# Attention and FFN on one core: the first unit's denominators at the end of a visit, VectorE's conversions, sums and transpositions between its slots

## The chip, the cores and the metric

The kernel runs on one core of one Trainium2 chip. Its inputs and outputs are fp32. The metric is the device time of one execution in microseconds (us), of which several runs are taken; their median is compared.

## The reference

Attention with normalized queries and keys over 8 batches of 12 heads, 448 tokens and 64 channels a head, and behind it a feed-forward network (FFN) with a squared ReLU over all 3584 tokens:

```python
def rmsnorm(x, g):
    return x / np.sqrt(np.mean(x * x, axis=-1, keepdims=True) + 1e-06) * g
q_n, k_n = rmsnorm(q, g_q), rmsnorm(k, g_k)
scores = 1.0 / np.sqrt(q.shape[-1]) * np.matmul(q_n, k_n.transpose(0, 1, 3, 2))
attn = np.exp(scores - np.max(scores, axis=-1, keepdims=True))
attn = attn / (np.sum(attn, axis=-1, keepdims=True) + 1e-09)
attn_out = np.matmul(attn, v)                                # (8, 12, 448, 64)
x = attn_out.transpose(0, 2, 1, 3).reshape(8 * 448, 12 * 64) # (3584, 768)
h = np.maximum(x @ w_in, 0.0)                                # w_in (768, 2048)
out = h * h @ w_out                                          # w_out (2048, 768)
```

## The kernel before, in words

**Pairs and units.** The attention is worked off in 48 pairs, each of one batch and two heads. Two batches (12 pairs, 896 tokens) make a unit, and each unit is followed by its share of the FFN. While the attention of a unit runs, TensorE also works on the FFN of the unit before it: the FFN's matmuls are a stream (a generator) that is stepped in portions between the *visits* of the attention. Up to pair 12 a pair has two visits, and there is little to fill in between. From pair 13 on there is one visit per pair, `visit_whole(i)` (L1826). The visits 13 to 24, beside which the stream of the first FFN runs, are the "first unit" here: `first` is true in them.

**One visit.** Visit `i` finishes pair `i-1` and begins pair `i`. It has three slots, one per chunk of 128 keys. In each, TensorE multiplies pair `i-1`'s weights with the values (`attend_halves`, L569, eight matmuls) and then makes pair `i`'s scores (`score`, L451, eight matmuls); ScalarE takes the exponentials from the bank to the tiles `wT` (`weigh`, L470). The 64 keys that are left over (448 = 3·128 + 64) are done for two pairs at once: in even visits their scores (L462), in odd visits their share of the result (`attend_both`, L590). ScalarE and VectorE join the two halves of the result in `xT` (`join_halves`: L580 and L581 on ScalarE, L578 or L582 on VectorE).

**Denominators.** GpSimd adds the weight tiles of a pair to a tile `sum` (`add_up`, L489); these additions are queued behind the visit in which the weights were made. In the next visit, as its first step, `denominators(i-1)` multiplies the two sums with ones (L624, four matmuls) into the bank that `sums_bank` names, and `take_sums` has VectorE transpose that bank to the tile `inverse` (L666). The bank is bank 2. The slots' scores go to banks (0, 1), (2, 0) and (1, 2) (`banks_of`, L439), so the second slot needs bank 2 back and waits for L666. Behind the visit the tasks `invert` (VectorE, L683 and L684) and `finish` (GpSimd, L712) divide `xT`.

**What runs between the visits.** `run` (L1631) takes one step of the FFN's stream at a time: a product of six matmuls of L1025 in the first half of a block (`first_products`), matmuls of L1290 and L1204 in the second. With each it does one *deep step* (a difference or sum of parts of the weights that VectorE makes, L1516, and that SP stores; the first of these steps only stores five raw parts, L1506 and L1508), one weight sum (`make_sum`, L1556, in turn on VectorE and GpSimd), `end_join` (VectorE, L1480), some tasks, and when it is due a conversion: `convert` (L1562) has SP load a piece of the weights into one of three tiles `words` (L1428, L1433), ScalarE split it (L1447, L1448, L1450) and VectorE join it in two steps (L1461, L1480). A `words` tile comes free when L1480 has read it; a load for which none is free holds up SP and all that is queued behind it. The four tiles `more` of the deep steps come free when SP's stores (L1534) have read them.

**SP's queue.** Transfers for the attention stand in a queue of their own in the program, `transfers`, of which `follow_transfers` sends two (or some more, as the queue is longer) with each step of the stream (L333): queries and keys (`load_qk`), queries brought to another order through DRAM, values `vt` and `lasts` (`load_v`).

**Transpositions and their scaling.** `turn_blocks` (L371) transposes the next pair's keys and queries on VectorE (L374), and ScalarE scales the queries (`scale_turned`, L384). These tasks are queued ahead of the visit, two per visit; what is left of them is run at the visit's start. While `closing` is true the scaling waits until the visit's end.

Of the kernel before, what the change touches and what calls it, by code (L numbers as in the profile page):

```python
# [26 lines left out]
NJ = 3  # L27
# [198 lines left out]
def program(ctx, tc, rows, v, g, wide, ones, moe_w_in, moe_w_out, out, shift):  # L226
# [3 lines left out]
    B, H, S, D = v.shape  # L230
# [46 lines left out]
    def whole(i):  # L277
        return i > 2 * NPAIR

    def by_two(i):  # L280

        return i >= 2 * 2 * NPAIR
# [21 lines left out]
    def alone(i):  # L304

        return pairs[i][0] < 2
# [76 lines left out]
            dst = to_scale.popleft()  # L383
            nc.scalar.mul(dst, dst, g)  # L384

    to_scale, closing = deque(), False

    def load_v(i):
        b, c = pairs[i]
# [136 lines left out]
                nc.vector.tensor_copy(out=tiles[NJ][e][mine, part], in_=tr[mine, NJ, :size])  # L526

    def sums_bank(i):
        return banks[4 + (i + 1) % 2 if alone(i) else 2 if whole(i + 1) else 3][:, 0:S]

    def values_bank(i):
# [1294 lines left out]
    def visit_whole(i):  # L1826
        nonlocal closing
        late = [some for some in tasks if getattr(some, "args", None) == (i,)]
        for some in late:
            tasks.remove(some)  # L1830
        run_all()
        if shift:
            attend_all(i - 1)
            if i <= last:
                weigh_slots(i, 1)
        else:
            if not by_two(i - 1):
                denominators(i - 1)
            elif i % 2 == 0:
                both_denominators(i - 2)  # L1840
            for n in range(NJ):
                attend(i - 1, (n,))
                forget(i - 1, (n,))
                if i <= last:
                    score(i, n)
                    weigh(i, n)
                while n == 1 and i % 2 == 0 and late:
                    late.pop(0)()
            if i % 2:
                attend(i - 1, (NJ,))  # L1850
                forget(i - 1, (NJ,))
            join_halves(i - 1)
            if not by_two(i - 1):
                tasks.append(lambda: invert(i - 1))
                tasks.append(lambda: finish(i - 1))
            elif i % 2 == 0:
                tasks.append(lambda: invert_both(i - 2))
            if i % 2 == 0:
                if i <= last:
                    score(i, NJ)  # L1860
                    weigh(i, NJ)
            if i <= last:
                additions(i)
        closing = False
        scale_turned()
        tasks.extendleft(reversed(late))
        if late:
            tasks.extendleft([gap] * 3)
        if shift or i % 2:
            prepare(i + 3)  # L1870
        else:
            tasks.append(lambda: tasks.append(lambda: prepare(i + 3, 0)))
        if i <= last:
            tasks.appendleft(lambda: load_v(i))
# [7 lines left out]
    with tc.manual_schedule(engines=ENGINES):  # L1882
# [8 lines left out]
        for i in range(len(pairs) + 1):  # L1891
            for n in range(1 if whole(i) else VISITS):
# [7 lines left out]
                run(place(u, x - (1 if whole(i - 1) else 0.5)))  # L1900
                if i < last:
                    if whole(i) and not shift:
                        tasks.append(partial(lambda i: turn_blocks(i + 1, 1), i))
                        tasks.append(partial(lambda i: turn_blocks(i + 1, 0), i))
                        tasks.append(partial(lambda i: load_qk(i + 4), i))
                    else:
                        for some in (1, 0) if whole(i) else (1 - n,):
                            turn_among(i + 1, some)
                        if n or whole(i):
                            tasks.append(lambda i=i: load_qk(i + 4))  # L1910
                    if n and first and x > 1 and not shift:
                        denominators(i - 1)
# [49 lines left out]
```

## Time and profile before

| | |
|---|---|
| times of three runs, us | 1408.22, 1413.85, 1414.09 (median 1413.85) |
| profiled execution, us | 1409.54, of which its span is 1407.4 |
| busy TensorE matmul | 1352.2 us, 96% of the span |
| busy VectorE, ScalarE, GpSimd | 823.2, 619.2 and 807.1 us |
| DMA | 229.85 MB, mean 163 GB/s |

The profile is of one execution; its times are in microseconds from the start of its span. PE is TensorE's matmul, DVE is VectorE, ACT is ScalarE, POOL is GpSimd, SPq is the queue in which SP issues DMAs. In a row of the timeline stand the start, the duration of the group, engine, line and operation, the tiles written and read, the shape and the number of instructions; in brackets the idle time before them and what ended it. In a row of the list of waits stand the engine and line that waited, for whom, the microseconds in total, how often, and the longest one. In a row of the table of stretches stand the stretch and its length, then the busy time (and number of instructions) of PE, of its weight loads, of DVE, ACT and POOL, then the granted clock of TensorE (1.00 is full), DMA's busy share and GB/s. Visit 13 stands at 140 us in the profile, visit 24 at 483 us, and a visit comes every 28 to 38 us between them.

### The profile page before, as it was taken

Reading aid. Unit: us, or ns where it says so; the run is one execution under the profiler, and the core shown is the slowest. Engines: PE = TensorE matmul, PEld = TensorE weight load, DVE = VectorE, ACT = ScalarE, POOL = GpSimd, SP = SyncE. Lnnn points to the kernel's source line nnn. Section 1 sums busy time; section 2 is a strip of 40 time slices with the busy share of each in tenths; the row PEclk is TensorE's granted clock in tenths of the full one; section 3 lists DMA queues with packets and bytes.
Section 4 is the critical chain, followed back from the end, with each engine's and each line's share of the span. In section 5 each row is a group of like instructions: output and inputs, shape, how many; then the busy total and the mean of one; then the engine's idle time right before and its main releaser. Section 6 shows DMA issues by size and latency. Waiting matters only on the chain.

```text
span 1407.4 us, 20180 instructions
## 1 busy us (share of the span) xinstructions
PE 1352.2 (96%) x6608; PEld 855.0 (61%) x6608; DVE 823.2 (58%) x1647; ACT 619.2 (44%) x1136; POOL 807.1 (57%) x804
## 2 busy tenths in 40 slices
PE   7997999899899899999999999999999999999998
PEld 3332455354344458585867667676858686868684
DVE  4897446676566775455555775555545742444444
ACT  6994567656657324343334434343433132303030
POOL 5668656565546696576576888567545740303030
PEclk9999999999999999999999999999999999999999
DMA  5665746767767858384756766584717361616133
GB/s 140 162 186 147 198 107 159 227 193 187 213 172 222 245 160 254 80 232 115 190 144 162 240 172 201 123 223 94 235 33 258 113 207 38 199 38 199 38 124 103
DMA packets 394374, 229.85 MB, mean 163 GB/s; under 512 B 271892, under 2 KB 355988, under 8 KB 393236
## 3 DMA queue, kind: packets, MB, share of 16 engines
q1 hardware_dynamic: 393968, 228.41, 57.7%
q8 instruction: 54, 0.88, 0.3%
q14 instruction: 60, 0.49, 0.1%
q10 hardware_dynamic: 292, 0.07, 0.0%
HBM read 171.05 MB, written 57.34 MB: 162 GB/s over the span
## 4 chain that ended last, share of the span: by engine, by line
PE 78%; DVE 8%; issue 4%; DMA 3%; POOL 3%; SPq 2%; ACT 1%; POOLq 0%; DVEq 0%; ACTq 0%
PE bank L1290 29%; PE bank L1081 25%; PE bank L451 6%; PE bank L569 6%; PE bank L1025 4%; PE bank L462 2%; PE bank L1204 2%; DVE acc L1387 1%; PE bank L590 1%; PE bank L554 1%; PE bank L624 1%; PE bank L633 1%; POOL rr L204 1%; DVE more L1516 1%; DVE out_sb L1480 1%
## 5 line engine op out<-in xcount | busy, mean ns | idle before, releaser
L1081 PE MATMUL bank<-xT,in_sb 128*128 128x224 f32 x1344 | 287.9, 353 | 0.1
L1290 PE MATMUL bank<-out_sb,hid 128*128 128x384 f32 x768 | 275.3, 490 | 12.4 <-DVE acc L1387 9.8
L1081 PEld LDWEIGHTS bank<-xT,in_sb 128*128 128x128 f32 x1344 | 252.9, 190 | 10.5 <-ACT wT L470 5.8
L1387 DVE TENSOR_TENSOR acc<-acc,bank 128x384 f32<-128x384 f32 x312 | 165.7, 547 | 129.6 <-PE bank L1290 118.7
L470 ACT ACTIVATE wT<-bank,rr 128x448 f32<-128x448 f32 x288 | 165.3, 631 | 155.6 <-PE bank L451 140.1
L1290 PEld LDWEIGHTS bank<-out_sb,hid 128*128 128x128 f32 x768 | 144.6, 190 | 115.8 <-DVE acc L1387 15.1
L1290 PE MATMUL bank<-out_sb,sums 128*128 128x384 f32 x576 | 207.9, 492 | 2.5 <-DVE acc L1387 2.0
L204 POOL TENSOR_TENSOR rr<-ms,minus_half 128x8 f32<-128x8 f32 (+1 forms) x96 | 146.3, 1524 | 64.7 <-DVE ms L197 62.1
L1290 PEld LDWEIGHTS bank<-out_sb,sums 128*128 128x128 f32 x576 | 108.4, 191 | 87.4 <-issue 5.5
L1066 DVE TENSOR_TENSOR hid<-hid,bank 128x224 f32<-128x224 f32 x312 | 111.3, 383 | 84.1 <-PE bank L1081 78.8
L451 PE MATMUL bank<-qT,kT 64*64 64x448 f32 x840 | 119.6, 551 | 10.1 <-DVE inverse L666 8.6
L1025 PE MATMUL bank<-xT,in_sb 128*128 128x448 f32 x336 | 128.7, 542 | 0.0
L489 POOL TENSOR_TENSOR sum<-sum,wT 128x448 f32<-128x448 f32 (+1 forms) x96 | 114.7, 1213 | 1.9
L489 POOL TENSOR_TENSOR sum<-wT 128x448 f32<-128x448 f32 x48 | 53.7, 1138 | 108.0 <-ACT wT L470 108.0
L569 PE MATMUL bank<-wT,vt 64*64 64x448 f32 x864 | 113.4, 551 | 0.0
L1025 PEld LDWEIGHTS bank<-xT,in_sb 128*128 128x128 f32 x336 | 63.1, 190 | 66.5 <-issue 65.2
L1134 POOL TENSOR_TENSOR hid<-hid 128x448 f32<-128x448 f32 x24 | 27.3, 1143 | 123.2 <-DVE hid L1066 118.2
L1138 ACT ACTIVATE hid<-hid 128x448 f32<-128x448 f32 x96 | 55.0, 573 | 72.0 <-DVE hid L1066 48.1
L582 DVE TENSOR_TENSOR xT<-xT,bank 128x448 f32<-128x448 f32 x36 | 22.4, 621 | 102.1 <-ACT xT L581 99.5
L451 PEld LDWEIGHTS bank<-qT,kT 64*64 64x64 f32 x840 | 45.8, 134 | 55.8 <-issue 38.2
L384 ACT ACTIVATE qT<-qT,g 128x448 f32<-128x448 f32 x34 | 22.6, 665 | 121.3 <-DVE qT L374 121.3
L1081 PE MATMUL bank<-more,in_sb 128*128 128x224 f32 x288 | 74.4, 353 | 0.0
(142 smaller groups left out, 2091.8 us busy)
## 6 DMA issues: line engine op xcount, KB each, us to landing
out_sb<-out_forms SPq DMA_DIRECT2D x80, 384.0 KB, 4.9
in_sb<-in_deep SPq DMA_DIRECT2D x64, 384.0 KB, 4.0
in_sb<-in_deep SPq DMA_DIRECT2D x80, 256.0 KB, 3.9
words<-in_moe_w_in_dram SPq DMA_DIRECT2D x32, 384.0 KB, 3.6
words<-in_moe_w_out_dram SPq DMA_DIRECT2D x32, 384.0 KB, 3.7
out_forms<-out_sb SPq DMA_DIRECT2D x8, 1536.0 KB, 6.5
qk<-in_q_dram SPq DMA_DIRECT2D x96, 96.0 KB, 2.7
qk<-in_k_dram SPq DMA_DIRECT2D x96, 96.0 KB, 2.6
```

Of the source, the lines that this page charges most:

```text
L204: self.nc.gpsimd.tensor_tensor(out=self.rr[i][:, x, 0 : self.count(i)], in0=ms, in1=self.minus_half.to_broadcast(list(ms.shape)), op=ALU.pow,)
L451: nc.tensor.matmul(sc[ds(half * D, D)], lhsT=turned[i, 1][ds(e * D, D), ds(m * P + half * D, D)], rhs=turned[i, 0][ds(e * D, D), :], start ...
L462: nc.tensor.matmul(sc[some], lhsT=turned[p, 1][r, keys], rhs=turned[p, 0][r, :], start=True, stop=True,)
L470: nc.scalar.activation(new_weights((i, m), e), sc, AF.Exp, scale=rows.rr[i][:, 1, 2 * m + e : 2 * m + e + 1],)
L489: nc.gpsimd.tensor_tensor(out=sums[i, e][some], in0=left[some], in1=weights[key_of(i, m), e][some], op=ALU.add)
L569: nc.tensor.matmul(bank[ds(e * D, D), :], lhsT=values[i][keys, n, e, :], rhs=weights[(i, n), e][keys], start=n == 0, stop=n == NJ - 1 and ...
L1025: nc.tensor.matmul(ps, lhsT=w_sb[:, IN.index(left), c, :], rhs=forms[u, c][right], start=first and c == 0, stop=c == NK - 1, skip_group_ch ...
L1066: nc.vector.tensor_tensor(out=quarter(name, n), in0=quarter(base, n), in1=ps, op=ALU.add)
L1081: nc.tensor.matmul(ps, lhsT=left, rhs=right, start=start, stop=stop, skip_group_check=True)
L1138: nc.scalar.activation(dst, dst, AF.Relu)
L1290: nc.tensor.matmul(ps, lhsT=extra[left][:, t] if tt == NT else lefts[left][:, t, ts(tt, P)], rhs=w_sb[t][:, OUT.index(right), :], start=fi ...
L1387: nc.vector.tensor_tensor(out=acc, in0=acc, in1=ps, op=ALU.add)
```

## The change

In the first unit's visits, and there only:

1. `sums_bank` names bank 1 for the denominators in place of bank 2.
2. `denominators(i-1)`, that is L624 on TensorE and L666 on VectorE, stands at the end of the visit in place of its start: in even visits behind the leftover keys' scores, in odd ones behind L590. The tasks `invert` and `finish` are queued behind it.
3. A conversion that has begun may take its first VectorE step (L1461) at the visit's start, unless it is the first piece of its tile; and behind each of the three slots stand `end_join` (L1480), one deep step and one weight sum.
4. In the odd visits 15 to 23, the transpositions for the next pair stand behind the first and second slot in place of ahead of the visit; the scaling on ScalarE follows at the end of the visit. The loads of `load_qk(i+4)` are queued behind the visit, ahead of `load_v(i)`.

The tiles, their buffers, the arithmetic and the number of instructions stay as they are. The lines of the changed kernel are 2 higher from `sums_bank` on (L1025 is L1027 there, L624 is L626, L666 is L668), and some more behind `visit_whole`.

```diff
-    to_scale, closing = deque(), False
+    to_scale, closing, in_visit = deque(), False, deque()
...
     def sums_bank(i):
+        if whole(i + 1) and not by_two(i):
+            return banks[1][:, 0:S]
         return banks[4 + (i + 1) % 2 if alone(i) else 2 if whole(i + 1) else 3][:, 0:S]
...
         else:
-            if not by_two(i - 1):
-                denominators(i - 1)
-            elif i % 2 == 0:
+            if i % 2 == 0 and by_two(i - 1):
                 both_denominators(i - 2)
+            if first and begun and all_pieces[begun[0]][2]:
+                join_words(begun.pop())
             for n in range(NJ):
                 attend(i - 1, (n,))
                 forget(i - 1, (n,))
...
                 while n == 1 and i % 2 == 0 and late:
                     late.pop(0)()
+                if n < 2 and in_visit:
+                    in_visit.popleft()()
+                if first:
+                    end_join()
+                    if deep_to_make:
+                        deep_to_make.popleft()()
+                    make_sum()
             if i % 2:
                 attend(i - 1, (NJ,))
                 forget(i - 1, (NJ,))
             join_halves(i - 1)
+            if i % 2 == 0:
+                if i <= last:
+                    score(i, NJ)
+                    weigh(i, NJ)
             if not by_two(i - 1):
+                denominators(i - 1)
                 tasks.append(lambda: invert(i - 1))
                 tasks.append(lambda: finish(i - 1))
...
-                        tasks.append(partial(lambda i: turn_blocks(i + 1, 1), i))
-                        tasks.append(partial(lambda i: turn_blocks(i + 1, 0), i))
-                        tasks.append(partial(lambda i: load_qk(i + 4), i))
+                        steps = [
+                            partial(lambda i: turn_blocks(i + 1, 1), i),
+                            partial(lambda i: turn_blocks(i + 1, 0), i),
+                        ]
+                        loads = partial(lambda i: load_qk(i + 4), i)
+                        if first and i % 2 and x < unit:
+                            in_visit.extend(steps)
+                            closing = True
+                        else:
+                            tasks.extend([*steps, loads])
+                            loads = None
...
                     visit_whole(i)
+                    if i < last and not shift and loads:
+                        tasks.appendleft(loads)
```

How the instructions stand on an engine shows what this does to the order. First TensorE at visit 13; `bank_172` to `bank_176` are the banks 0 to 4. Before:

```order
L1025 MATMUL bank_178<-xT,in_sb 128x448 x3
L624 MATMUL bank_174<-sum,ones 64x448 x2
L569 MATMUL bank_176<-wT,vt 64x448 x2
L569 MATMUL bank_175<-wT,vt 64x448 x2
L451 MATMUL bank_172<-qT,kT 64x448 x2
...
L451 MATMUL bank_174<-qT,kT 64x448 x2
L590 MATMUL bank_176<-wT,lasts_156 64x448 x2
L590 MATMUL bank_172<-wT,lasts_157 64x448 x2
L1025 MATMUL bank_177<-xT,in_sb 128x448 x3
```

The same place of the changed kernel:

```order
L1027 MATMUL bank_178<-xT,in_sb 128x448 x3
L571 MATMUL bank_176<-wT,vt 64x448 x2
L571 MATMUL bank_175<-wT,vt 64x448 x2
L451 MATMUL bank_172<-qT,kT 64x448 x2
...
L451 MATMUL bank_174<-qT,kT 64x448 x2
L592 MATMUL bank_176<-wT,lasts_156 64x448 x2
L592 MATMUL bank_172<-wT,lasts_157 64x448 x2
L626 MATMUL bank_173<-sum,ones 64x448 x2
L1027 MATMUL bank_177<-xT,in_sb 128x448 x3
```

The denominators (L624, now L626) have moved from ahead of the slots to behind them, directly ahead of the FFN's next matmuls, and from bank 2 to bank 1.

Then VectorE at visit 17, an odd one; `words` are pieces under conversion, `more` are deep steps. Before:

```order
L1516 TENSOR_TENSOR more<-in_sb 128x512
L1480 ISA out_sb<-words,out_sb 128x768
L1461 TENSOR_SCALAR out_sb<-words 128x384
L1167 TENSOR_TENSOR hid<-bank_178,part 128x448
L1516 TENSOR_TENSOR more<-in_sb 128x512
L1556 TENSOR_TENSOR out_sb<-out_sb 128x384
L1480 ISA out_sb<-words,out_sb 128x768
L666 STREAM_TRANSPOSE inverse<-bank_174 128x448
L582 TENSOR_TENSOR xT<-xT,bank_175 128x448
L1516 TENSOR_TENSOR more<-in_sb 128x384
```

The same place of the changed kernel:

```order
L1463 TENSOR_SCALAR out_sb<-words 128x384
L374 STREAM_TRANSPOSE kT<-qk_65 128x448
L1482 ISA out_sb<-words,out_sb 128x768
L1518 TENSOR_TENSOR more<-in_sb 128x384
L374 STREAM_TRANSPOSE qT<-qk_65 128x448
L1518 TENSOR_TENSOR more<-in_sb 128x384
L584 TENSOR_TENSOR xT<-xT,bank_175 128x448
L668 STREAM_TRANSPOSE inverse<-bank_173 128x448
L1169 TENSOR_TENSOR hid<-bank_177,part 128x448
L685 RECIPROCAL few<-inverse 128x14
```

The transposition of the sums (L666, now L668) stood ahead of the join of the halves and behind a conversion's end; now it stands behind the join of the halves (L582, now L584), and five other instructions stand ahead of that join, within the visit.

Last SP between the visits 16 and 17. Before:

```order
L1433 DMA words<-in_moe_w_out_dram 128x768
L333 DMA qk_65<-q_rows 32x14x32 x2
L1433 DMA words<-in_moe_w_out_dram 128x768
L333 DMA qk_65<-q_rows 32x14x32 x2
L1506 DMA in_deep_161<-in_sb 896x1x128 x3
L1508 DMA in_deep_161<-in_sb 896x1x128 x2
L333 DMA vt<-in_v_dram 128x3x64 x2
L1433 DMA words<-in_moe_w_out_dram 128x768
```

The same place of the changed kernel:

```order
L333 DMA q_rows<-qk_65 128x3x128
L1508 DMA in_deep_161<-in_sb 896x1x128 x3
L1510 DMA in_deep_161<-in_sb 896x1x128 x2
L333 DMA q_rows<-qk_65 64x128 x2
L1435 DMA words<-in_moe_w_out_dram 128x768 x2
L333 DMA qk_65<-q_rows 32x14x32 x3
L1536 DMA in_deep_161<-more 128x4x128
L333 DMA qk_65<-q_rows 32x14x32
L333 DMA vt<-in_v_dram 128x3x64
```

The five stores of the raw parts (L1506 and L1508, now L1508 and L1510), which stood behind two loads of weight pieces (`words`) and directly ahead of the values `vt` of visit 17, now stand ahead of those two loads; the transfers of queries are mixed in differently.

More of the change, by code (lines that the diff above doesn't have):

```diff
@@ L1857, in visit_whole @@
                 tasks.append(lambda: invert_both(i - 2))
[L1858 to L1861, printed above, removed]
             if i <= last:
```

## The prediction

> **What bounds the kernel now.** The page says how long the profiled execution is, and the table of stretches, read next, says which engine fills it in each stage.
>
> ```profile
> span 1407.4 us, 20180 instructions
> ```
>
> ```profile
> core 0: us, PE busy (x) PEld busy (x) DVE busy (x) ACT busy (x) POOL busy (x), PEclk, DMA share, GB/s
> 0.00:130.00 130.00, 117.99 (x720) 46.15 (x721) 99.23 (x237) 100.72 (x183) 84.07 (x79) 1.00 0.62 163
> 130.00:515.00 385.00, 350.28 (x1457) 172.49 (x1459) 252.14 (x434) 222.36 (x385) 241.42 (x204) 0.97 0.69 188
> 515.00:1098.00 583.00, 580.46 (x3232) 411.80 (x3224) 328.44 (x681) 239.46 (x454) 399.34 (x431) 1.00 0.61 171
> 1098.00:1407.40 309.40, 303.43 (x1214) 224.57 (x1208) 143.43 (x297) 56.67 (x114) 82.23 (x93) 1.00 0.36 118
> ```
>
> TensorE fills every stage. The change touches the second row alone, the visits 13 to 24, and there TensorE idles 385.0 − 350.28 = 34.7 us, and the mean granted clock is 0.97 where the others have 1.00. So the stage can give back at most some 35 us and what the lower clock costs. The list of waits of TensorE for this stage says for whom it idles:
>
> ```profile
> PE bank L1290 <- DVE acc L1387: 11.2, 10, 2.6
> PE bank L624 <- POOL sum L489: 8.7, 1, 8.7
> PE bank L451 <- DVE inverse L666: 8.6, 3, 3.1
> PE bank L1290 <- POOL out_sb L1556: 2.2, 2, 1.5
> PE bank L1204 <- ACT hid L1174: 2.1, 2, 1.4
> PE bank L451 <- ACT wT L470: 1.4, 1, 1.4
> ```
>
> One wait of 8.7 is at the denominators (L624, visit 13), three are at scores that wait for the transposition of the sums (L666), and the rest is spread over the FFN's second products (L1290). Those are three different things, and each is costed by itself. Last, the stretches in which the granted clock falls:
>
> ```profile
> 136.90:143.70 6.80, 3.21 (x8) 0.88 (x12) 2.89 (x4) 0.00 (x0) 6.72 (x7) 0.50 0.59 157
> 259.80:263.20 3.40, 3.40 (x22) 1.49 (x14) 0.00 (x0) 1.86 (x4) 2.22 (x2) 0.50 1.10 334
> 283.70:287.10 3.40, 3.40 (x7) 1.89 (x6) 3.40 (x8) 2.43 (x4) 3.32 (x3) 0.50 0.98 249
> 355.40:362.10 6.70, 6.01 (x28) 1.90 (x28) 2.78 (x6) 3.59 (x7) 2.71 (x3) 0.50 0.98 264
> 481.70:485.00 3.30, 3.30 (x10) 0.82 (x14) 1.59 (x3) 0.00 (x0) 3.30 (x4) 0.50 1.18 275
> ```
>
> Each follows one of the waits and doubles the time of the matmuls in it, so it costs half of their busy time: 1.7 in each of the short ones, 6.01 / 2 = 3.0 in the one of 6.70.
>
> **The change part by part: visit 13.** The timeline of TensorE around it, and GpSimd's sums:
>
> ```profile
> 126.99 4.78 PE L1025 MATMUL bank<-xT,in_sb 128*128 128x448 f32 x12
> 140.49 2.84 PE L624 MATMUL bank<-sum,ones 128*64 128x448 f32 x4 [8.72 <-POOL sum L489]
> 143.26 1.19 PE L569 MATMUL bank<-wT,vt 64*64 64x448 f32 x8
> ...
> 149.16 1.02 PE L1025 MATMUL bank<-xT,in_sb 128*128 128x448 f32 x2
> ```
>
> ```profile
> 136.68 4.83 POOL L489 TENSOR_TENSOR sum<-sum,wT 128x448 f32<-128x448 f32 x4
> ```
>
> TensorE is done at 131.77 and waits for the sums, though the visit's own 56 matmuls, behind L624, don't need them. They take 149.16 − 143.26 = 5.9. In the changed order they run from 131.8 to 137.7, and the denominators follow when the last sum is there, at 136.68 + 4.83 = 141.5, with about 0.7 for the half that needs it. The FFN goes on at 142.2 in place of 149.16: 7.0 at most. The idle time of about 3 us now stands behind the visit, and if it still brings a half clock, that is 1.7: 5.3, which I take; a price for the next visit's values stands below. The lower end is 7.0 − 3.4 = 3.6, with two such windows.
>
> *A page's rule beside this.* The Trainium skill, "TensorE: Matmul & The Clock Gate", Part 1, has the clock fall after a whole idle window of about 3.4 us that runs freely, and rise after a busy one. By it the wait of 8.7 must bring a low window and one of 3 us need not; the sum would then be 1.7 better. The trace agrees only in part: the rows above have 0.50 after waits of 3.1 us and less, the clock's stretches are 3.3 to 3.4 or twice that.
>
> **The waits for L666, visits 17, 20 and 23.** Removed is the need of the second slot for the bank that L666 empties. What comes next there is the exponentials, and these are the rows (ScalarE and TensorE at visit 17, then at 20 and 23):
>
> ```profile
> 256.25 0.55 ACT L1447 ACTIVATE words<-words 128x384 f32<-128x384 f32 x1 [1.36 <-DMA words<-in_moe_w_out_dram]
> ...
> 258.08 2.41 ACT L470 ACTIVATE wT<-bank,rr 128x448 f32<-128x448 f32 x4
> ```
>
> ```profile
> 258.29 1.06 PE L451 MATMUL bank<-qT,kT 64*64 64x448 f32 x6 [3.13 <-DVE inverse L666]
> ```
>
> ```profile
> 355.43 1.66 ACT L470 ACTIVATE wT<-bank,rr 128x448 f32<-128x448 f32 x3
> ```
>
> ```profile
> 353.68 0.97 PE L451 MATMUL bank<-qT,kT 64*64 64x448 f32 x4 [2.47 <-DVE inverse L666]
> ```
>
> ```profile
> 450.36 1.14 ACT L470 ACTIVATE wT<-bank,rr 128x448 f32<-128x448 f32 x2
> ```
>
> ```profile
> 451.95 0.98 PE L451 MATMUL bank<-qT,kT 64*64 64x448 f32 x8 [3.02 <-DVE inverse L666]
> ```
>
> At stake are 3.13 + 2.47 + 1.44 (the wait for L470 in the list) + 3.02 = 10.1, and the low clock behind the first two, 1.7 + 3.0 = 4.7; together 14.8. But the first slot's exponentials begin at 258.08, 0.2 ahead of TensorE's going on at 258.29: ScalarE stands on a conversion whose words came late. With L666 gone, the second slot still needs the bank that these exponentials empty (bank 0). At visit 20 they start 1.75 after the resumption, at 23 the first is over 1.0 before it. So alone the move is worth 0 to 1.2 there. The rest hangs on whether the words come earlier. In the changed order the five raw stores leave SP ahead of two loads of words and not between them and the next, and VectorE's end of a conversion, which frees a `words` tile, may come in a visit. I take half, 7.4, between 1.2 and 14.8; the half because one of the three visits (23) isn't late on ScalarE, and of the other two I expect one to be relieved.
>
> **The FFN's waits for VectorE, GpSimd and ScalarE.** 11.2 + 2.2 + 2.1 = 15.5, and the low clocks at 283.7 and 481.7, 1.7 each: 18.9. VectorE has time in the visits to take work off the stretches between them:
>
> ```profile
> DVE xT L582 <- ACT xT L581: 35.3, 6, 6.5
> DVE xT L578 <- PE bank L569: 19.0, 6, 4.3
> ```
>
> That is 54.3 us of idling in twelve visits, 4.5 in one. The groups give the price of what moves in:
>
> ```profile
> L1480 DVE CUSTOM_DVE_ANT_0 out_sb<-words,out_sb 128x768 uint16<-128x768 uint16 x24 | 19.9, 830 | 0.0
> L1516 DVE TENSOR_TENSOR more<-in_sb 128x512 f32<-128x512 f32 (+1 forms) x24 | 19.5, 814 | 0.5 <-DMA in_deep<-more 0.5
> ...
> L1556 DVE TENSOR_TENSOR out_sb<-out_sb 128x384 f32<-128x384 f32 x12 | 10.7, 889 | 0.0
> ```
>
> One end of a conversion, up to three deep steps and one or two sums: 0.83 + 3 · 0.81 + 1.5 · 0.89 = 4.6, about what the idling holds. Deep steps exist only in some visits, so most hold less. But the products wait where L1387 is late by about 1 us at a time (11.2 in ten waits), at the second products after visits 15, 18, 21 and 24, and the conversions there have their own due times, which the change leaves. I take a third, 6.3, between 0 and 18.9.
>
> **What it costs.** At visit 17, one VectorE operation beside a sum of GpSimd was long:
>
> ```profile
> 254.54 1.44 POOL L1190 TENSOR_TENSOR sums<-hid,sums 128x384 f32<-128x384 f32 x1
> ```
>
> ```profile
> 255.05 1.34 DVE L1556 TENSOR_TENSOR out_sb<-out_sb 128x384 f32<-128x384 f32 x1
> ```
>
> That is half more than the group's mean. What is moved ends ahead of the join (L582 or L578), which is needed only by `finish`; it may be late by 1 us without cost. In even visits the leftover scores and in odd ones L590 stand between the last scores and the denominators, so L624 in bank 1 finds the third slot's exponentials nearly done; if not, it costs under 1 us a visit.
>
> *A page's rule that speaks against the change.* "SBUF — State Buffer", section "Who interferes with whom", of the Trainium skill says that a VectorE instruction with two inputs in SBUF contends with a GpSimd instruction that reads SBUF, and that one blocks the other wholly. By it the sums and deep steps in the visits, where GpSimd adds weights, would take up to twice as long, 0.8 us more each, so that a visit's 4.6 would be up to 9 and pass its idling of 4.5. The 1.34 agrees; that it costs TensorE anything no row shows, and my sum goes without it.
>
> The loads of `load_qk` now stand ahead of the values of the visits 16, 18, 20, 22 and 24, and raw stores or deep steps elsewhere. Two rows of SP, TensorE's start of visit 24 and the values' time from issue to landing, from the view of the tile `vt`:
>
> ```profile
> 158.70 1.77 SPq L333 DMA_DIRECT2D vt<-in_v_dram  x2
> ```
>
> ```profile
> 477.40 0.49 SPq L333 DMA_DIRECT2D vt<-in_v_dram  x1
> ```
>
> ```profile
> 483.22 1.76 PE L624 MATMUL bank<-sum,ones 128*64 128x448 f32 x4
> ```
>
> ```profile
> DMA to landing us min/median/max: 2.5/3.7/6.2
> ```
>
> Issued at 477.4, the last values of visit 24 land by the median at 481.1 and by the longest at 483.6; they are needed behind L624, at 483.22 + 1.76 = 485.0, before and, without L624 ahead of them, at 483.2 now. Four loads more, sent two with each product, are two products of 2.4 (twelve matmuls in 4.78): 4.8 us. That makes a wait of 481.1 + 4.8 − 483.2 = 2.7 if the stream doesn't hold the slack. The values of visit 14, issued at 158.7, are sent with the products behind visit 13 and move ahead with them. I take 3 in all, between 0 and 13.
>
> **Sum.** 5.3 + 7.4 + 6.3 − 3 = 16 off the profiled execution's 1409.54, which is its span and 2.1 around it: 1393.5. The runs shown lie 1.3 below it and 4.3 and 4.6 above it; the mean of all four is 1411.4, the median of the three 1413.85. I shift by the middle, 3 us: 1396.5.
>
> **The rivals.** *The stage is paced by SP and its DMAs.* The stage has the highest DMA share, 0.69, the values land just ahead of their visits, and ScalarE waits for words at 256.25. Then the waits move to the values and words, and only visit 13's 3.6 to 5.3 is gained, less some of the cost: 1409.5 − 4.5 + 2 = 1407, with the shift 1410. Against it: the waits by name are for VectorE, not for DMAs. Chance 0.2.
>
> *Slower: the values come behind the queries and keys.* If visits 18, 20 and 24 each wait for `vt`, at 4.8 less a slack of 0 to 2, some 3.5 each, and each brings a low clock of 1.7, that is 15.6; with visit 13's 5.3 gained and nothing else 1409.5 + 10.3 = 1420, with the shift 1423. It decides where the values' slack falls under 4.8; for it speaks visit 24's, against it that SP has time in the stretches between (it sends more as its queue grows). Chance 0.11.
>
> *A larger gain: ScalarE and the words are relieved too.* Then the second term is worth 13 and the third 10: 1409.5 − 5.3 − 13 − 10 + 2 = 1383, with the shift 1386. Chance 0.14.
>
> **How the numbers follow.** The forecast has 0.55. Half a per cent, 7 us, is about what a measurement of this kernel tells from no change. Faster by more is the forecast and the larger gain, 0.69; within it is the pacing by SP, 0.2; slower is the third, 0.11. The terms' ends reach from 1384 to 1410 with the shift. The range from 1386 to 1410 leaves out the slower case and half of the larger gain.
>
> **What would show it.** Right: no wait at L624 ahead of visit 13 (L626 there waits 3 us behind the slots) and the FFN's matmuls 5 to 7 us earlier; no score waits for the transposition of the sums; the second row of the table of stretches some 16 us shorter at a clock of 0.98 or more. Wrong: L451 waiting for L470, or L569 for `vt`, at visits 17 to 24 as long as before for L666; the waits of L1290 for L1387 still about 11; the stage as long as now in spite of the start.

## The result and the profile after

| | before | after |
|---|---|---|
| runs, us | 1408.22, 1408.70, 1413.85, 1414.09 | 1391.81, 1392.53, 1392.73, 1394.64 |
| median, us | 1411.28 | 1392.63 |
| profiled execution (span), us | 1409.54 (1407.4) | 1392.53 (1390.7) |

The changed kernel takes 0.987 of the time of before, 95% interval 0.984 to 0.990: 18.7 us less by the medians, 17.0 by the profiled executions. The stage of the visits 13 to 24 ended at 515.0 before, 0.5 behind the start of visit 25; in the changed kernel the same place is at 497.5. Its row of the table of stretches, and the waits of TensorE in it:

```profile
130.00:497.50 367.50, 346.88 (x1457) 171.23 (x1459) 246.64 (x434) 222.14 (x385) 237.73 (x204) 0.98 0.72 197
```

```profile
PE bank L1292 <- POOL out_sb L1558: 8.9, 3, 4.2
PE bank L451 <- ACT wT L470: 4.5, 3, 2.7
PE bank L1292 <- DVE acc L1389: 3.3, 5, 1.2
PE bank L1027 <- DVE hid L1169: 2.4, 2, 2.0
PE bank L626 <- POOL sum L489: 1.4, 2, 0.8
```

The stage is 17.5 us shorter, and the idle time of TensorE in it is 367.5 − 346.9 = 20.6 in place of 34.7. That is 14.1 less. The stretches at a granted clock of 0.50 are these now:

```profile
280.90:284.30 3.40, 3.40 (x14) 1.09 (x18) 1.75 (x4) 0.00 (x0) 0.00 (x0) 0.50 1.06 403
345.70:349.10 3.40, 3.17 (x20) 1.29 (x24) 2.31 (x4) 1.86 (x4) 0.33 (x1) 0.50 0.37 105
461.80:468.60 6.80, 5.54 (x26) 1.96 (x28) 0.86 (x2) 0.60 (x2) 4.79 (x6) 0.50 0.83 273
```

They hold 12.1 us of matmuls in place of 19.3, and half of that is what they cost, so 3.6 less than before. The waits have changed their names, too: no score waits for L666 (L668 now), and the waits for L1387 (L1389) have gone from 11.2 to 3.3, but those for weight sums on GpSimd have risen from 2.2 to 8.9 and those for L470 from 1.4 to 4.5, and one for L1169 is new.

Where the time went is seen best by when each visit starts, read off TensorE's timeline (the first of its small matmuls) and compared with before. Here is that difference in us, minus for earlier, for the changed kernel and all experiments below:

| start of visit | 14 | 17 | 18 | 20 | 21 | 23 | 24 | 25 |
|---|---|---|---|---|---|---|---|---|
| before, at us | 167.4 | 251.8 | 290.1 | 347.8 | 386.4 | 445.5 | 483.2 | 514.5 |
| after | −3.0 | −2.6 | −7.8 | −7.9 | −11.1 | −13.6 | −18.6 | −17.5 |
| e1_end_only | −5.5 | −4.6 | −0.7 | −0.7 | +1.2 | +1.3 | +2.8 | +3.0 |
| e2_tasks_only | −0.3 | −0.5 | −7.3 | −6.7 | −10.7 | −13.3 | −17.7 | −17.6 |
| e3_no_turns | −3.0 | −1.6 | −5.1 | −6.1 | −10.7 | −13.2 | −16.4 | −16.0 |
| e4_deep13 | −5.3 | −5.0 | −10.5 | −9.8 | −12.9 | −15.5 | −18.5 | −17.9 |
| e5_sums_deep | +0.9 | +0.8 | −1.4 | −1.4 | −6.8 | −6.8 | −9.6 | −8.9 |
| e6_joins | −0.2 | −0.2 | +0.7 | −0.4 | −1.9 | −3.4 | −3.5 | −3.3 |
| e7_raw_last | +1.0 | +0.9 | +5.8 | +5.8 | +9.1 | +9.1 | +7.6 | +13.3 |
| e8_sums_dve | −5.7 | −4.9 | −13.6 | −14.5 | −20.4 | −23.0 | −31.5 | −32.4 |
| f1_dve_alone | +0.8 | +0.6 | +2.3 | +2.3 | +1.5 | +1.5 | +3.0 | +3.9 |
| f2_scale_late | −5.3 | −4.8 | −13.3 | −14.3 | −20.9 | −23.4 | −32.4 | −33.2 |
| f3_start_dve | +1.2 | +1.1 | −7.4 | −8.4 | −15.2 | −17.8 | −25.6 | −26.5 |
| f4_raw_act | +0.1 | +1.1 | +1.8 | +2.2 | −0.3 | +1.0 | +2.7 | +3.4 |

Visit 13 in the changed kernel, on TensorE:

```profile
131.57 0.98 PE L571 MATMUL bank<-wT,vt 64*64 64x448 f32 x8
...
136.25 0.59 PE L451 MATMUL bank<-qT,kT 64*64 64x448 f32 x2 [1.45 <-ACT wT L470]
...
140.39 0.97 PE L626 MATMUL bank<-sum,ones 128*64 128x448 f32 x2 [0.81 <-POOL sum L489]
141.93 0.96 PE L626 MATMUL bank<-sum,ones 128*64 128x448 f32 x2 [0.57 <-POOL sum L489]
142.82 11.54 PE L1027 MATMUL bank<-xT,in_sb 128*128 128x448 f32 x30
156.42 5.14 PE L1027 MATMUL bank<-xT,in_sb 128*128 128x448 f32 x12 [2.05 <-DVE hid L1169]
```

The wait of 8.7 ahead of the visit is gone, and the FFN goes on at 142.8 in place of 149.2, 6.3 earlier. The idle time that is left, 1.45 + 0.81 + 0.57 = 2.8, stands half within the slots and half at L626, and no low clock follows it. But half of the 6.3 is given back before visit 14: at 156.42 the products wait for VectorE. Its timeline there has the cause, a deep step that waits for a `more` tile until SP's store has read it:

```profile
145.38 0.62 DVE L1169 TENSOR_TENSOR hid<-bank,part 128x448 f32<-128x448 f32 x1 [1.26 <-PE bank L1027]
153.86 0.69 DVE L1518 TENSOR_TENSOR more<-in_sb 128x512 f32<-128x512 f32 x1 [7.85 <-DMA in_deep<-more]
```

### The profile page after: what moved, and what is told of

Its sections match the earlier page's. It is cut to its first block, busy times and chain, and to the rows that moved or that the text cites. A ratio compares the mean times of both kernels' runs of the same rounds, so it can differ in the third digit from the quotient of the medians.

```text
span 1390.7 us, 20191 instructions
## 1 busy us (share of the span) xinstructions
PE 1349.6 (97%) x6608; PEld 853.8 (61%) x6608; DVE 818.0 (59%) x1647; ACT 618.9 (45%) x1136; POOL 803.1 (58%) x804
## 4 chain that ended last, share of the span: by engine, by line
PE 81%; DVE 6%; DMA 4%; POOL 3%; issue 3%; SPq 2%; ACT 1%; POOLq 0%; ACTq 0%; DVEq 0%
PE bank L1292 30%; PE bank L1083 25%; PE bank L451 6%; PE bank L571 6%; PE bank L1027 5%; PE bank L1206 2%; PE bank L462 2%; PE bank L556 1%; PE bank L592 1%; DVE acc L1389 1%; SPq L333 1%; PE bank L635 1%; PE bank L626 1%; POOL out_sb L1558 1%; PE bank L608 1%
## 5 line engine op out<-in xcount | busy, mean ns | idle before, releaser
L1389 DVE TENSOR_TENSOR acc<-acc,bank 128x384 f32<-128x384 f32 x312 | 166.1, 548 | 132.3 <-PE bank L1292 123.9
L470 ACT ACTIVATE wT<-bank,rr 128x448 f32<-128x448 f32 x288 | 165.1, 631 | 143.8 <-PE bank L451 127.8
L1292 PEld LDWEIGHTS bank<-out_sb,hid 128*128 128x128 f32 x768 | 144.8, 190 | 113.9 <-POOL out_sb L1558 10.7
L1027 PE MATMUL bank<-xT,in_sb 128*128 128x448 f32 x336 | 129.5, 543 | 2.5 <-DVE hid L1169 2.4
L451 PE MATMUL bank<-qT,kT 64*64 64x448 f32 x840 | 121.1, 550 | 4.5 <-ACT wT L470 4.5
L489 POOL TENSOR_TENSOR sum<-sum,wT 128x448 f32<-128x448 f32 (+1 forms) x96 | 111.3, 1179 | 2.0
L1027 PEld LDWEIGHTS bank<-xT,in_sb 128*128 128x128 f32 x336 | 62.8, 190 | 69.1 <-issue 62.3
L451 PEld LDWEIGHTS bank<-qT,kT 64*64 64x64 f32 x840 | 46.2, 136 | 52.6 <-issue 39.9
L1080 ACT COPY hid<-bank 128x448 f32<-128x448 f32 x24 | 12.8, 532 | 137.2 <-PE bank L1083 137.2
```

What stands on the lines that cost most here:

```text
L451: nc.tensor.matmul(sc[ds(half * D, D)], lhsT=turned[i, 1][ds(e * D, D), ds(m * P + half * D, D)], rhs=turned[i, 0][ds(e * D, D), :], start ...
L470: nc.scalar.activation(new_weights((i, m), e), sc, AF.Exp, scale=rows.rr[i][:, 1, 2 * m + e : 2 * m + e + 1],)
L489: nc.gpsimd.tensor_tensor(out=sums[i, e][some], in0=left[some], in1=weights[key_of(i, m), e][some], op=ALU.add)
L1027: nc.tensor.matmul(ps, lhsT=w_sb[:, IN.index(left), c, :], rhs=forms[u, c][right], start=first and c == 0, stop=c == NK - 1, skip_group_ch ...
L1292: nc.tensor.matmul(ps, lhsT=extra[left][:, t] if tt == NT else lefts[left][:, t, ts(tt, P)], rhs=w_sb[t][:, OUT.index(right), :], start=fi ...
L1389: nc.vector.tensor_tensor(out=acc, in0=acc, in1=ps, op=ALU.add)
```

## The experiments

Each ratio is to runs of the kernel before on the same chip. Its median there is 1410.00 us for e1 to e4, 1409.16 for e5 to e8 and 1410.40 for f1 to f4, so medians of runs from different groups can differ by about 1 us for this reason alone.

**e1_end_only.** From the changed kernel:

```diff
-                if n < 2 and in_visit:
-                    in_visit.popleft()()
-                if first:
-                    end_join()
-                    if deep_to_make:
-                        deep_to_make.popleft()()
-                    make_sum()
...
-            if first and begun and all_pieces[begun[0]][2]:
-                join_words(begun.pop())
...
-                        if first and i % 2 and x < unit:
+                        if False:
```

> The denominators at the end of the visit and in bank 1, and nothing else of the change: VectorE's tasks, the transpositions and the loads stay between the visits. Theory A (three separate terms): visit 13 ends 6 to 7 us earlier as in the changed kernel, and keeps it, since no deep steps stand in the visit; at visits 17, 20 and 23 the scores wait for the exponentials (L470) in place of L666 and recover at most 1 us each; the FFN's waits stay. In all 7 to 9 us less than before, about 1403. Theory B (the order on TensorE and the bank are the whole gain, the tasks in the visits bring nothing): as fast as the changed kernel, 1390 to 1394.

Measured: 1414.17 us against 1410.00, ratio 1.0029 (1.0018 to 1.0040): slower. Visit 14 starts 5.5 earlier and visit 17 still 4.6; there the lead goes. The scores there wait for L470 in place of L666, and longer. TensorE and ScalarE at visit 17, the stretch of low clock that follows, and the wait in the list:

```profile
255.45 1.01 PE L451 MATMUL bank<-qT,kT 64*64 64x448 f32 x2 [5.10 <-ACT wT L470]
```

```profile
252.95 0.55 ACT L1449 ACTIVATE words<-words 128x384 f32<-128x384 f32 x1 [2.48 <-DMA words<-in_moe_w_out_dram]
...
254.78 1.66 ACT L470 ACTIVATE wT<-bank,rr 128x448 f32<-128x448 f32 x3
```

```profile
254.40:261.20 6.80, 5.75 (x28) 1.73 (x28) 0.00 (x0) 3.94 (x7) 0.00 (x0) 0.50 0.93 272
```

```profile
PE bank L451 <- ACT wT L470: 14.9, 5, 5.1
```

The words come 3.3 us earlier than before (252.95 against 256.25), the visit starts 4.6 earlier, so it waits longer, and the low clock behind it lasts 6.8 in place of 3.4. Both theories are wrong on the sum: the order on TensorE isn't the gain (B), and it doesn't keep its own term either (A).

**e2_tasks_only.** The opposite half. From the changed kernel:

```diff
-        if whole(i + 1) and not by_two(i):
-            return banks[1][:, 0:S]
...
-            if i % 2 == 0 and by_two(i - 1):
+            if not by_two(i - 1):
+                denominators(i - 1)
+            elif i % 2 == 0:
                 both_denominators(i - 2)
...
-                denominators(i - 1)
                 tasks.append(lambda: invert(i - 1))
```

> VectorE's tasks in the visits, the transpositions between slots and the loads behind the visit as changed, but the denominators at the visit's start and in bank 2 as before. Theory A: the 8.7 us wait of visit 13 stays; the waits for L666 at visits 17, 20 and 23 get shorter by some, since VectorE has less in front of L666 and the words come earlier; 3 to 6 us less than before, 1405 to 1408. Theory B: no gain, 1411 within 3.

Measured: 1392.35 us, ratio 0.9873 (0.9856 to 0.9889): the whole gain of the changed kernel (0.987). Its waits of TensorE in the stage:

```profile
PE bank L1290 <- POOL out_sb L1556: 8.9, 3, 4.2
PE bank L624 <- POOL sum L489: 8.7, 1, 8.7
PE bank L1290 <- DVE acc L1387: 3.3, 5, 1.2
PE bank L451 <- DVE inverse L666: 2.2, 2, 1.9
```

The 8.7 stands, as said, but the waits for L666 are down from 8.6 to 2.2 with bank 2 and the visit's start as before. So they were not a matter of bank or place: VectorE and the words were late. Both theories are off: A had 1405 to 1408, B no gain. These waits sum to 23.1, 2.6 more than after, though the time is the same. The low clock doesn't make up for that: its stretches hold 13.1 us of matmuls here and 12.1 after. But TensorE is busy 2.6 us longer in the changed kernel with the same matmuls, and 3.1 without what the low clock costs; 1.4 of that lies within visit 13 and 0.8 in the stretch behind it. What makes it longer was not settled.

**e3_no_turns.** The changed kernel with `if False:` in place of the condition that puts the transpositions into odd visits.

> The changed kernel with the transpositions (L374) and the scaling (L384) of the odd visits ahead of the visit again, and the loads of queries and keys in their old place. Theory A: the scaling stands ahead of the exponentials on ScalarE again, so visits 17 and 23 lose 0.5 to 1.5 us each; the values' slack grows, which no wait asks for: 1392 to 1396. Theory B: no change from the changed kernel, 1392.6 within 1.5.

Measured: 1393.45 us, ratio 0.9885 (0.9867 to 0.9902). The interval holds the changed kernel's ratio, and the median lies in both expected ranges, so the two theories are not told apart; by the profile the stage is 1.5 longer, and L451 waits more for L470, 5.9 in place of 4.5. These 1.5 are not the price of the transpositions alone: e3 happens to have one stretch of low clock, of 3.4 us, where the changed kernel has 13.6 us of it. The loads in their old place, ahead of the visit, bring nothing that could be seen: neither kernel has a wait for `vt`.

**e4_deep13.** The changed kernel with `if deep_to_make and i > 13:` in the slots.

> The changed kernel without the deep steps in visit 13 alone; they are made between the visits as before. Theory A: the products behind visit 13 (L1027) no longer wait for VectorE (L1169), which idled 7.9 us for a store of a deep step; of the 3.3 us that the changed kernel gives back between visits 13 and 14 some 2.5 to 3.3 stay gained: 1389 to 1390.5. Rival: the deep steps wait for the same stores when they are made between the visits, and nothing is gained: 1392.6 within 1.

Measured: 1390.77 us, ratio 0.9853 (0.9837 to 0.9870), which overlaps with the changed kernel's; the median lies between the two expected ranges. In the profile the cause is confirmed:

```profile
142.66 16.05 PE L1027 MATMUL bank<-xT,in_sb 128*128 128x448 f32 x42
159.60 2.52 PE L1027 MATMUL bank<-xT,in_sb 128*128 128x448 f32 x6 [0.89 <-DVE hid L1169]
```

42 matmuls run without a break, and visit 14 starts 5.3 earlier and not 3.0. But of these 2.3 only 0.4 are left at visit 25. The lead won early melts at the later visits that are held by something else: against e2 it is 5.0 at visit 14, 3.2 at visit 18 and 0.3 at visit 25.

**e5_sums_deep and e6_joins.** The tasks taken apart, both from e2_tasks_only and with transpositions and loads as before: e5 has in the slots only the deep step and `make_sum()`, e6 only `end_join()` (and the `join_words` ahead of them).

> Of the tasks in the visits only the weight sum and the deep step behind each slot; conversions, transpositions, loads and denominators as before. Theory C (SP's queue: the deep steps begin a few products earlier, so that their five raw stores leave SP while it idles, and the words behind them and with them the exponentials of visits 17, 20 and 23 are no longer late): 12 to 18 us less than before, 1392 to 1398. Theory D (VectorE's ends of conversions in the visits free the tiles of words earlier): at most 3 us less, 1407 to 1411.

> Of the tasks in the visits only the two VectorE steps of a conversion; sums, deep steps, transpositions, loads and denominators as before. Theory C: at most 3 us less than before, 1407 to 1411. Theory D: 10 to 17 us less, 1393 to 1400.

Measured: e5 1398.91 us against 1409.16, ratio 0.9931 (0.9912 to 0.9950); e6 1406.80, ratio 0.9981 (0.9967 to 0.9994). By the start of visit 25 they win 8.9 and 3.3 of the 17.6. D falls; C holds in direction, not in size. Two rows of e5's waits, then one of e6's:

```profile
PE bank L1290 <- DVE acc L1387: 8.4, 11, 1.4
...
PE bank L451 <- DVE inverse L666: 6.5, 3, 2.6
```

```profile
PE bank L451 <- DVE inverse L666: 7.4, 3, 3.1
```

Neither half clears the waits for L666 (8.6 before, 2.2 with everything). The 5.4 that are missing come from the transpositions in the visits or from the parts together; which, was not taken further apart.

One thing can be read off their traces, though. In the visits 17, 20 and 23 themselves, from start to end, e5 wins 7.7 and e6 nothing (0.1 longer), of the 11.4 of e2. And only e5 sends the raw stores earlier: ahead of visit 17 they begin at 226.70, in e6 at 238.42, as before (238.61). That fits theory C for these three visits.

**e7_raw_last.** From the kernel before:

```diff
-        return [raw] + [lambda make=make: both(make) for make in steps + [None, None]]
+        return [lambda make=make: both(make) for make in steps + [None, None]] + [raw]
```

> The kernel before with one edit: the five raw stores of the deep steps (L1506, L1508) are issued as the last of their block's steps in place of the first. Nothing moves on VectorE, ScalarE or TensorE. Theory C: the words behind them come some 5 us earlier at visits 17, 20 and 23, and most of the 14.8 us of waits and low clock there goes: 7 to 14 us less than before, 1396 to 1403, if the stores don't hold up the words or values of the visits 18, 21 and 24 where they now stand. Theory D: no change, 1410 within 2.

Measured: 1423.61 us, ratio 1.0103 (1.0075 to 1.0130): slower. Within the visits 17, 20 and 23 themselves, from the visit's start to its end, 1.6 + 5.2 + 1.1 = 7.9 us are won, as C said. But the stretches after the visits 17 and 20 lose 6.5 and 8.6, and visit 24 loses 5.7: its last values, issued at 489.75 behind the raw stores, come too late (L569 waits 1.5 for them), and the clock is at 0.50 for 10.2 us there. C's condition, that the stores hold up nothing where they now stand, isn't met. The waits of VectorE, and TensorE's longest one in the first of these stretches:

```profile
DVE in_sb L1461 <- DMA in_deep<-in_sb: 18.1, 2, 10.3
```

```profile
288.51 2.93 PE L1290 MATMUL bank<-out_sb,hid 128*128 128x384 f32 x4 [8.46 <-DVE acc L1387]
```

A conversion of w_in (L1461) writes a tile `in_sb` that the raw stores still read. So these stores have two duties: they must be out of the way of words, and they must be done before the next tile of w_in is begun. Issued earlier, as in the changed kernel, they meet both: VectorE has no wait for `in_deep<-in_sb` there.

**e8_sums_dve.** The largest wait of the changed kernel is for weight sums on GpSimd. They stand in its queue behind other work, while VectorE idles (GpSimd, then TensorE and VectorE of the changed kernel ahead of visit 24):

```profile
459.09 2.02 POOL L204 TENSOR_TENSOR rr<-ms,minus_half 128x8 f32<-128x8 f32 x1
461.07 1.94 POOL L1558 TENSOR_TENSOR out_sb<-out_sb 128x384 f32<-128x384 f32 x2
```

```profile
463.06 1.65 PE L1292 MATMUL bank<-out_sb,hid 128*128 128x384 f32 x2 [4.17 <-POOL out_sb L1558]
```

```profile
464.75 0.56 DVE L1313 TENSOR_TENSOR acc<-acc,bank 128x384 f32<-128x384 f32 x1 [4.14 <-PE bank L1292]
```

From e4_deep13:

```diff
-            next(sum_engines).tensor_tensor(out=to, in0=left, in1=right, op=op)
+            engine = nc.vector if len(to.shape) == 2 else next(sum_engines)
+            engine.tensor_tensor(out=to, in0=left, in1=right, op=op)
```

> The changed kernel without deep steps in visit 13 (the fourth run), and all weight sums of w_out on VectorE in place of every second on GpSimd. In the changed kernel L1292 waits 8.9 us for such sums on GpSimd, behind its other work, while VectorE idles. If the place on GpSimd is what is late, these 8.9 go and some of the low clock behind them: 1382 to 1387. Rival: the sums are late because they are taken up late, and VectorE's own backlog grows (L1389): 1390 within 2.

Measured: 1378.22 us against 1409.16, ratio 0.9778 (0.9755 to 0.9802), below the expected range. The stage and its waits:

```profile
130.00:482.50 352.50, 341.69 (x1454) 171.55 (x1456) 250.12 (x446) 222.70 (x385) 225.99 (x192) 1.00 0.75 205
```

```profile
PE bank L451 <- ACT wT L470: 4.6, 3, 3.2
PE bank L1292 <- DVE acc L1389: 3.9, 7, 1.2
PE bank L1027 <- DVE hid L1169: 0.9, 1, 0.9
PE bank L626 <- POOL sum L489: 0.8, 1, 0.8
PE bank L1292 <- DVE out_sb L1559: 0.4, 1, 0.4
```

The 8.9 are gone, TensorE idles 10.8 us, and the granted clock is 1.00 throughout: the low clock goes with the waits.

**f1_dve_alone.** The same edit on the kernel before.

> The kernel before with one edit: all weight sums of w_out on VectorE. If GpSimd's sums cost what the waits of before show for them, 2.2 us, and VectorE has no room for them between the visits: 0 to 3 us less or more than before, 1407 to 1412. If the sums on GpSimd are what makes the whole chain of weights late, in the kernel before too: 8 to 13 us less, 1396 to 1401.

Measured: 1410.14 us against 1410.40, ratio 0.9998 (0.9984 to 1.0013). No gain. Two rows of its waits:

```profile
PE bank L1290 <- DVE acc L1387: 11.0, 10, 2.6
...
PE bank L451 <- DVE inverse L666: 7.4, 3, 2.7
```

GpSimd's 2.2 are gone from its waits, but those for VectorE stay (L1387 had 11.2 before): VectorE was already what is late. The edit pays only where the tasks in the visits have given VectorE room.

**f2_scale_late.** From e8_sums_dve, behind `loads = None`:

```diff
+                            closing = first and x < unit
```

In this kernel the leftover scores of the odd pairs, which stand in the even visits, are made from queries that aren't scaled yet; the work is the same, so its time can be read, but it is no version to use.

> The eighth run (changed kernel, no deep steps in visit 13, sums of w_out on VectorE) with the scaling of the queries (L384) behind the even visits too. There visit 20 still waits 3.2 us for an exponential that stands behind the scaling on ScalarE. If the scaling is what is late: 2.5 to 4 us less than that run, 1374 to 1376. If the words ahead of it are as late: within 1 us, 1377 to 1379.

Measured: 1376.60 us, ratio 0.9765 (0.9740 to 0.9789). Of TensorE's waits, the one for L470 falls from 4.6 to 1.9, and another takes its place at the leftover scores:

```profile
PE bank L462 <- DVE xT L580: 1.9, 1, 1.9
PE bank L451 <- ACT wT L470: 1.9, 3, 1.0
```

By the start of visit 25 this is worth 0.9; the medians' 1.6 are inside the intervals, and the median lies between the two expected ranges. The scaling is little of what is left.

**f3_start_dve.** The sums' edit on e2_tasks_only, so that the denominators stand at the visit's start. From e8 it differs in two things, as e2 does from e4: the denominators' place and bank, and the deep steps, which visit 13 has here.

> The second run (tasks in the visits, denominators at the visit's start in bank 2) with the sums of w_out on VectorE: the eighth run without the denominators' move. Theory E (a lead won at visit 13 is lost only where a later stage is paced by the weights; without that pacing it stays): the 5.4 us of visit 13 and some 2 to 3 of waits for L666 are missing, 1383 to 1387. Rival: the denominators' place is worth nothing here either, 1378 to 1380.

Measured: 1382.28 us against 1410.40, ratio 0.9802 (0.9778 to 0.9826), 4.1 above e8_sums_dve by the medians. The intervals of the two ratios overlap by half, but the slowest run of e8 (1379.26) is faster than the fastest here (1381.82), and by the profile visit 25 comes 5.9 later here. Its first two waits are those that the move would take away:

```profile
PE bank L624 <- POOL sum L489: 8.3, 1, 8.3
PE bank L451 <- DVE inverse L666: 4.5, 3, 2.4
```

The median is 0.7 below theory E's range and 2.3 above its rival's, so E is the nearer one, and the table of visits bears it out: where the later stages no longer pace the stream, e8's lead over f3 stays (6.9 at visit 14, 6.0 at visit 17, 5.9 at visit 25), while e4's over e2 goes from 5.0 to 0.3.

**f4_raw_act.** The kernel before with `nc.scalar.dma_start` for the raw stores.

> The kernel before with one edit: the five raw stores are issued by ScalarE's DMA queue in place of SP's, at the same place of the program. Theory C (SP's queue): the words of visits 17, 20 and 23 come some 5 us earlier, the exponentials too, and the waits there fall from 10.1 to about 4 to 6: 5 to 10 us less than before, 1399 to 1405. Rival (the DMA traffic itself, or VectorE's backlog ahead of L666, makes these waits): within 3 us, 1407 to 1412.

Measured: 1412.23 us, ratio 1.0011 (0.9996 to 1.0026). No gain, but it doesn't decide against C: SP was freed (the values of visit 17 are issued at 238.59 in place of 244.60), but ScalarE, which makes the words' first step and the exponentials, stood still behind its own issues, and the waits for L666 rose to 11.1:

```profile
246.12 0.52 ACT L181 ACTIVATE squares<-qk 128x384 f32<-128x384 f32 x1 [4.97 <-issue]
```

## Why the prediction came out right, and where its steps were wrong

The time was forecast at 1396.5 and is 1392.6, inside the range, with the right sign. Its signs of being right came true as well: 6.3 at visit 13, no score that waits for L666, the stage 17.5 shorter at a clock of 0.98. They don't show the mechanism, since e2 is as fast with the wait of 8.7 still there. The terms, read off the table of visits:

- **Visit 13, forecast 5.3.** At the visit's end 6.3, as the order said, and without the low clock of 1.7 that was allowed for; at visit 14 only 3.0. The step that failed is that nothing behind the visit was asked for: the deep steps, put into its slots, fill the four `more` tiles and then hold VectorE for 7.9 us. With them out (e4) it is 5.3. And the term is worth nothing at the end: without it (e2) the stage ends at −17.6, with it at −17.5. No rival had this. The one in which SP and the words pace the stage is right that visits wait for words, but it kept just this term as its only gain, and a lead is what such visits swallow.
- **Visits 17, 20 and 23, forecast 7.4.** From the visits' starts and ends the changed kernel wins 4.22 + 2.82 + 3.23 = 10.3 there. "Removed is the need of the second slot for the bank" was the wrong cause: with that need kept, e2 wins 5.15 + 3.61 + 2.66 = 11.4, and with only that need removed (e1) 5.5 are lost. That the rest "hangs on whether the words come earlier" was the step that carried; the estimate of 0 to 1.2 for the move alone was too kind, since a visit that comes early to late words waits longer and pays a longer low clock.
- **The FFN's waits, forecast 6.3.** Between the visits 14 and 25 the stretches outside the visits get 6.6 shorter. The size is right, for another reason: the waits for L1387 fall by 7.9, much more than the third that was taken, but those for GpSimd's sums rise by 6.7, which the prediction didn't see, since the sums keep alternating between the engines and GpSimd's half stands behind other work in its queue. In all the waits of the second products fall from 15.9 to 12.2, by 3.7, and the low clock in these stretches costs 1.0 less. The other 1.9 are busy time of TensorE, whose cause the runs don't show.
- **The values, forecast −3.** No wait for `vt` appears. The other visits lose 2.4 in all, a cost that the sum didn't have: in 18 and 24, 1.0 and 1.1 of low clock at the waits for GpSimd's sums, and in 15 another 0.4 at full clock.
- **VectorE beside GpSimd.** The page's rule that speaks against the change, in "SBUF — State Buffer" of the Trainium skill, section "Who interferes with whom", is plain in visit 13 of the changed kernel, where GpSimd adds weights until 141.9 (VectorE, then GpSimd):

```profile
137.99 1.37 DVE L1518 TENSOR_TENSOR more<-in_sb 128x512 f32<-128x512 f32 x1
139.39 1.50 DVE L1518 TENSOR_TENSOR more<-more,in_sb 128x512 f32<-128x512 f32 x1
140.93 1.50 DVE L1518 TENSOR_TENSOR more<-in_sb,more 128x512 f32<-128x512 f32 x1
142.35 0.68 DVE L1518 TENSOR_TENSOR more<-in_sb 128x512 f32<-128x512 f32 x1
```

```profile
136.57 5.31 POOL L489 TENSOR_TENSOR sum<-sum,wT 128x448 f32<-128x448 f32 x4
```

The deep steps take twice as long beside GpSimd, which agrees with the rule. The sum took it that this costs TensorE nothing; that is not quite so. GpSimd is held up as well: its four sums take 5.31 in place of 4.83 before and 4.85 in e4, where only one deep step stands beside them. L626 waits a second time, 0.57, for the last of them, and in e4 it doesn't.

The shift of 3 us from the profiled execution to the median was too much: the changed kernel's median lies 0.1 above its profiled run. Of the 3.9 between forecast and result 2.9 are this shift, and only 1.0 the terms (16.0 forecast, 17.0 between the profiled executions). That the terms fit so well is in part luck: the 5.3 of visit 13 was not kept, the 3 for the values was not lost, and the visits 17, 20 and 23 gave 2.9 more than was taken. The range was too narrow for its own terms, too: with the ends given for each of them (3.6 to 7.0, 1.2 to 14.8, 0 to 18.9, a cost of 0 to 13) they reach from 1372 to 1421 with the shift, and not from 1384 to 1410.

Shown, then: the tasks in the visits are the gain. The denominators' move, with the deep steps out of visit 13, adds to it when GpSimd's sums are out of the way (5.9 by the profiles, e8 against f3) and hardly without that (0.3, e4 against e2). Argued, and not settled: how much of the gain is the raw stores' earlier place on SP. Within the visits 17, 20 and 23, moving them alone to the end wins 7.9 (e7) and e5, where they leave earlier, 7.7, of e2's 11.4. But no run moves them earlier alone, and f4, which frees SP of them, loads ScalarE and gains nothing.

## What to carry to other kernels

A wait that is removed early in a pipeline is a lead, not a gain: look which later stage is paced by something else, and count the term only if the lead gets past it. Name a wait by what is late, not by the bank or buffer that it names; keeping the buffer and moving the late engine's work told them apart here. And where work is pulled forward on an engine that shares it in turn with another, look at the other's queue: giving VectorE all sums of w_out was worth nothing in the kernel before (f1), and by the profiles 8.8 us (e2 to f3) and 14.5 (e4 to e8) where VectorE's tasks had moved into the visits.

## What the runs showed of the hardware

The granted clock falls in stretches of 3.4 us or a multiple (3.4, 6.8 and 10.2 in these runs), and the same wait may or may not bring one: 2.73 us at visit 20 of the changed kernel is followed by 0.50, 3.21 at the same visit of e8_sums_dve by none. The Trainium skill, "TensorE: Matmul & The Clock Gate", Part 1, has a freely running window of about 3.4 us; that would explain why like waits differ, but the wait of 2.73 is less than the whole idle window that it names. In f4 the raw stores kept ScalarE from working for 5.0 us ahead of visit 17; three of the five are issued in that time, which takes 1.1 and 2.4 us. VectorE's additions and subtractions of 128x512 from SBUF took 1.37 to 1.50 us beside GpSimd's additions and 0.68 right behind them, and GpSimd's four took 5.31 in place of 4.83.
